# Two more products of a fused attention and tanh-shrink layer computed in two levels, with their factors made on the way

## The chip, the cores and the metric

The kernel runs on one core of one Trainium2 chip. The metric is the device time of one execution in microseconds (us). Three runs of the kernel before took 666.34, 666.99 and 667.07 us; their median, 666.99 us, is the time before. All tensors are 32-bit floats.

## The reference, cut to what matters

```
# linear attention with decay, blocks of 64 along the sequence; B=4, H=8, S=768, D=64
intra = (q_b @ k_b^T * Dmask) @ v_b              # Dmask[i,j] = lam^(i-j) for i >= j
inter = (q_b * lam^(pos+1)) @ kv_state
out_b = intra + inter
kv_state = lam^block * kv_state + (k_b * lam^(block-1-pos))^T @ v_b
# then, on x = the heads side by side, 3072 rows x 512
h = x @ w_in                                     # 512 x 2048
g = h - tanh(h)
result = g @ w_out                               # 2048 x 512
```

The factor that multiplies k before it goes into the state (`lam^(block-1-pos)`) is called k's decay below.

## The kernel before, in words

The sequence is cut into six groups (g = 0 to 5) of 128 positions; with four batches a group has 512 rows, as four chunks b = 0 to 3. The kernel's own attention block is 128 positions.

**Products.** Both matrix products of the layer ("up", x @ w_in, and "down", g @ w_out) are done as seven products of half-size blocks instead of eight, P1 to P7, with sums and differences of blocks made beforehand and combined afterwards (`FACT` names the two operands of each). In `up(g, u, n)` (L449) product n of a quarter u of the hidden columns is four matmuls of 256 columns; the tanh and the subtraction follow in `finish`. `down(g, n)` (L622) is one product of the down projection as one level: 16 matmuls of 256 columns, in four steps u. `down_twice(g, n, zw)` (L675) does the same product in two levels: the block is cut in quarters again, and seven steps x = 1, 2, 6, 5, 7, 3, 4 of four matmuls of 128 columns are run, with three sums (s1, s2 and a21) made by `sums_twice` (L667) on VectorE, a fourth one (a12 -= s2, L691) between steps, a copy by ScalarE after steps 1, 6, 7 and 4 (L689), and two adds at the end (L696, L697). `TWICE` lists the products done in two levels: P3 to P7 of "down" in all groups from 1 on (P3 not in the last). P1 and P2 of "down" are one-level.

**Inner products.** From group 2 on (`GI = 2`), "up" P2 and P4 are done in two levels as well, for all four u at once, by `inner_steps` (L530): "in 2" and "in 4". They run at the end of the group before: "in 2" step by step in turn with the steps of "down" P3, then the stage called the **P4 stage** here: the steps of "in 4" with P1, P6 and P5 of u = 0 of the next group between them.

**Stages of a group from 2 on.** (1) "up" for u = 0 to 3, with the transposes of the next group's chunks 0 and 1 and, after "down" P1, their scores; (2) "down" P1 inside u = 3, then P2; (3) attention output and state of chunks 0 and 1; (4) "down" P4 and P5; (5) scores, P6, output and state of chunks 2 and 3; (6) P7, then P3 with "in 2", then the P4 stage.

**Attention.** `att_transpose` (L323) turns q and k by 32x32 transposes on VectorE (L331, from blocks that SyncE's DMA queue loads in 128-byte pieces, L143) and multiplies q by the powers of lam (L342); `att_scores` makes q k^T on TensorE and masks on VectorE (L356); `att_state` decays k on VectorE (`att_decay`, L361), multiplies by v, and updates the state with two VectorE operations (L379, L380); `att_out` (L384) multiplies state and scores. The PSUM results go to ScalarE (L410).

**Factors of w_out.** Group 0 computes the sums of w_out blocks and stores them to two tensors in memory: `factors` (one level) and `fine` (the second level for the five products of `TWICE`). Later each step loads its 256 KB factor by `piece` (L588), which GpSimd's DMA queue (POOL) issues in a fixed order (`stream`), up to seven (`RING = 7`) ahead; a load waits until the buffer of the seventh piece before it is free.

**Order of work.** A scheduler puts the instructions of each engine in an order; instructions wrapped in `tc.keep_in_program_order` (or `tied(True, ...)`) keep theirs. Each engine runs its queue in order. The banks of PSUM that matter: y banks `ya` and `yb`, `w`, `z`, one buffer each, and four for attention. The pool `sums` has four buffers.

Of the kernel before, what the change touches and what calls it, by code (L numbers as in the profile page):

```python
# [18 lines left out]
BLK = 128  # L19
GB = 2  # L20
# [4 lines left out]
def kernel(  # L25
# [91 lines left out]
    lam_blk = fwd[:, :, BLK - 1:BLK][:, None, :, :].to_broadcast([128, 2, NP, D])  # L117

# [67 lines left out]
    TWICE = (3, 5, 6, 4, 7)  # L186
# [65 lines left out]
    def sums_out(kt):  # L252
# [8 lines left out]
        for n, j in ((1, 0),) if kt % 2 == 0 else ((2, 0), (3, 1)):  # L261
            tied(kt > 1, nc.gpsimd.dma_start(out=fine[:, SUB.index(n), :, kt // 2, :].rearrange("n p c -> p n c"),
                                             in_=y[:, 1:6, ts(j, 128)]))
# [98 lines left out]

    def att_state(g, bs):
# [4 lines left out]
        for n, b in enumerate(bs):  # L368
            kd, vn = raw[g, b]["k"], raw[g, b]["v"]
            if g > 0:  # L370
                att_decay(g, b)
# [6 lines left out]
        if g > 0:  # L378
            nc.vector.tensor_tensor(st, st, lam_blk, op=AL.mult)  # L379
            nc.vector.tensor_tensor(st, st, kv, op=AL.add)  # L380
        else:
            tied(True, nc.scalar.activation(st, kv, AF.Copy))
# [66 lines left out]
    def up(g, u, n):  # L449
# [14 lines left out]
        def finish(c, src):  # L464
            th = work.tile([128, 2, HB], F32, name="th", tag="th")
            nc.scalar.activation(th, src, AF.Tanh)  # L466
# [6 lines left out]
        elif g >= GI and n == 5:  # L473
            nc.scalar.activation(dst(22), z, AF.Copy)
# [10 lines left out]
        elif n == 6:  # L485
            nc.scalar.activation(dst(12), y, AF.Copy)
# [15 lines left out]
    INNER = (2, 4)  # L502
    toks = {}
# [4 lines left out]
    def inner_weights(u):  # L508
        for n in INNER:
            a11, a12, a21, a22 = (a_quarter(n, u, i, k) for i in range(2) for k in range(2))  # L510
            t = late["pool"].tile([128, 4, 128], F32, name="ws2", tag="sums", bufs=4)
# [6 lines left out]
    def inner_tokens(g):  # L518
        for n in INNER:
            x = xt[g][FACT[n][1]]  # L520
            b11, b12, b21, b22 = (x[:, k, ts(j, 128)] for k in range(2) for j in range(2))
            t = late["pool"].tile([128, 4, 128], F32, name="tt2", tag="sums", bufs=4)
# [7 lines left out]
    def inner_steps(g, n, tag):  # L530
# [4 lines left out]
        for x in STEPS:  # L535
# [9 lines left out]
            if x in (1, 4, 6):  # L545
                nc.scalar.activation({1: c11, 4: c21, 6: c12}[x], d, AF.Copy)  # L546
            elif x == 5:
                nc.scalar.activation(r5, dst, AF.Copy)
# [12 lines left out]
    def twice(g, n):  # L561
        return n in TWICE and not (g == NG - 1 and n == 3)

# [7 lines left out]
    def pieces_of(g):  # L571
        if g >= GI:
            yield from ((g, ("in", 4), x) for x in (6, 5, 3))
# [13 lines left out]

    def piece(g, n, x):  # L588

        i = stream.index((g, n, x))  # L590
        while sent["n"] < min(i + RING, len(stream)):
            g_, n_, x_ = stream[sent["n"]]
            t = late["pool"].tile([128, 2, 256], F32, name="wb", tag="wb", bufs=RING)
            if isinstance(n_, tuple):
# [27 lines left out]
    def down(g, n):  # L622
# [16 lines left out]
        if n == 1:  # L639
            res[g, 1] = otile("q1")  # L640
            nc.scalar.activation(res[g, 1], t, AF.Copy)
        elif n == 4:
            res[g, 4] = otile("q4")
            nc.scalar.activation(res[g, 4], t, AF.Copy)
# [22 lines left out]
    def sums_twice(g, n):  # L667
        a11, a12, a21, a22 = quarter(g, n)
        s1, s2 = (late["pool"].tile([128, NU, 128], F32, name=f"s{x}", tag="sums", bufs=4) for x in (1, 2))
        nc.vector.tensor_tensor(s1, a21, a22, op=AL.add)  # L670
        nc.vector.tensor_tensor(s2, s1, a11, op=AL.subtract)
        nc.vector.tensor_tensor(a21, a11, a21, op=AL.subtract)
        low[g, n] = (s1, s2)

    def down_twice(g, n, zw):  # L675
        a11, a12, a21, a22 = quarter(g, n)
        s1, s2 = low.pop((g, n))
        y = bank("y2", "ya" if n in (4, 6, 3) else "yb", 1)[:, 0:128]
        zw = bank("zw", zw, 1)
        o = res[g, n] = otile(f"q{n}")  # L680
        for x, a, dst, keep in ((1, a11, y, o[:, 0:128]), (2, a12, zw[:, 0:128], None), (6, s2, y, o[:, 128:256]),
                                (5, s1, zw[:, 256:384], None), (7, a21, y, o[:, 384:512]), (3, a12, zw[:, 128:256], None),
# [5 lines left out]
            if keep is not None:  # L688
                nc.scalar.activation(keep, dst, AF.Copy)  # L689
            if x == 2:  # L690
                nc.vector.tensor_tensor(a12, a12, s2, op=AL.subtract)  # L691
# [6 lines left out]
        if n == 6:  # L698
# [18 lines left out]
    def down_end(g):  # L717
# [4 lines left out]
        for tag, m, c0, c1 in (("z", 0, 0, 256), ("w", 1, 0, 128), ("ya", 1, 128, 256)):  # L722
# [156 lines left out]
    up(1, 0, 1)  # L879
    for g in range(1, NG):  # L880
        last = g == NG - 1
        p0, p1 = attention(g + 1) if not last else ([], [])
        for u in range(NU):
            for n in (2, 6, 5, 7, 1, 4, 3) if g < GI else (1, 7, 3) if u == 0 else (6, 5, 1, 7, 3) if u + 1 < NU else (
# [5 lines left out]
                else:  # L890
                    every(down(g, 1))
                if g == 1 and u < 2 and n == 5:
                    sums_in(u + 2)
            if g == GI - 1:
                inner_weights(u)
            if not last and u > 1:
                run(p0[u - 2:u - 1])
        if twice(g, 4):
            sums_twice(g, 4)
        every(down(g, 2))  # L900
        run(p0[2:])
        sums_twice(g, 5)
        every(down_twice(g, 4, "z") if twice(g, 4) else down(g, 4))
# [3 lines left out]
        every(down_twice(g, 5, "w"))  # L907
        run(p1[1:2])
        if twice(g, 7):
            sums_twice(g, 7)  # L910
        every(down_twice(g, 6, "z"))
# [3 lines left out]
        every(down_twice(g, 7, "w") if twice(g, 7) else down(g, 7))  # L915
# [47 lines left out]
```

## Time and profile before

The profiled execution took 667.09 us, 0.10 above the median of the runs; its span on the core is 665.3 us, so 1.8 us lie outside the span.

| engine | busy us | share of the span | instructions |
|---|---|---|---|
| TensorE matmul (PE) | 653.6 | 98% | 4992 |
| TensorE weight load (PEld) | 594.6 | 89% | 4992 |
| VectorE (DVE) | 480.0 | 72% | 869 |
| ScalarE (ACT) | 215.0 | 32% | 413 |
| GpSimd (POOL) | 196.0 | 29% | 340 |

DMA moved 121.74 MB. One 32-bit matmul appears as two records in the profile, so the eight records of a step of "down" P3 to P7 are its four matmuls. Ends of matmuls are modelled and overlap the next start, so what a step takes is read from one start to the next, not from its duration. The busy share of an engine is a mean over stages with different limits; the stages around P1 and P2 are the ones to read here.

### The profile page before, as it was taken

What the parts mean: (1) busy time and instruction counts of PE and PEld (TensorE: products, weight loads), DVE (VectorE), ACT (ScalarE), POOL (GpSimd) and SP (SyncE); (2) the same over time, 40 slices, a digit from 0 to 9 for tenths busy, and PEclk for the clock granted to TensorE, in tenths of its full rate; (3) what the DMA queues carried; (4) which work ended last, traced back from release to release, by engine and by line L of the source; (5) the groups of instructions that cost most, each with busy time, mean ns of one, the idle gap of its engine ahead of it and who ended that gap; (6) DMA issues with size and microseconds to landing.
All of it is one profiled execution on the core that took longest, in us unless ns stands there. A gap on an engine that the chain in (4) does not pass through costs nothing.

```text
span 665.3 us, 13244 instructions
## 1 busy us (share of the span) xinstructions
PE 653.6 (98%) x4992; PEld 594.6 (89%) x4992; DVE 480.0 (72%) x869; ACT 215.0 (32%) x413; POOL 196.0 (29%) x340
## 2 busy tenths in 40 slices
PE   7899999999999999999999999999999999999998
PEld 6688888888888899888999988999988899988897
DVE  4467888997787994579895379887368877357753
ACT  4787933423321112341112342112243112233110
POOL 0001425783112445001435101254300245400261
PEclk9999999999999999999999999999999999999999
DMA  9999946997346979435899643698830676610495
GB/s 209 221 209 255 282 159 198 349 332 221 81 87 150 268 214 292 81 71 115 219 265 273 149 76 72 164 297 247 218 68 16 160 237 216 222 38 1 114 303 169
DMA packets 161006, 121.74 MB, mean 183 GB/s; under 512 B 133872, under 2 KB 135024, under 8 KB 160944
## 3 DMA queue, kind: packets, MB, share of 16 engines
q0 software_dynamic: 26400, 86.27, 41.0%
q1 hardware_dynamic: 134400, 34.64, 26.0%
q8 instruction: 39, 0.64, 0.4%
q14 instruction: 23, 0.19, 0.1%
q10 hardware_dynamic: 144, 0.00, 0.0%
HBM read 100.67 MB, written 20.19 MB: 182 GB/s over the span
## 4 chain that ended last, share of the span: by engine, by line
PE 74%; issue 9%; DVE 6%; DMA 4%; POOL 3%; SPq 2%; ACT 2%; POOLq 0%; DVEq 0%; ACTq 0%
PE y L458 13%; PE y L686 12%; PE zw L686 9%; PE z L458 8%; PE h L741 7%; PE y L542 4%; PE w L633 4%; PE y L633 4%; PE sp L352 3%; PE op L406 2%; PE z L542 2%; PE op L400 1%; PE w L542 1%; PE end L725 1%; DMA fine<-wt 1%
## 5 line engine op out<-in xcount | busy, mean ns | idle before, releaser
L598 POOL DMA_DIRECT2D wb<-fine x168 | 90.5, 538 | 137.3 <-PE y L686 60.8
L466 ACT ACTIVATE th<-g 128x512 f32<-128x512 f32 x76 | 47.6, 630 | 99.5 <-DVE g L471 34.2
L689 ACT ACTIVATE q<-y 128x128 f32<-128x128 f32 x96 | 26.6, 278 | 149.3 <-PE y L686 148.5
L458 PE MATMUL y<-xt,w 128*128 128x256 f32 x320 | 73.5, 380 | 0.0
L601 POOL DMA_DIRECT2D wb<-factors x44 | 23.8, 542 | 165.0 <-PE y L633 127.8
L458 PEld LDWEIGHTS y<-xt,w 128*128 128x128 f32 x320 | 59.9, 190 | 8.5 <-ACT g L546 0.9
L467 DVE TENSOR_TENSOR g<-g,th 128x512 f32<-128x512 f32 x76 | 52.1, 689 | 21.1 <-ACT th L466 21.0
L686 PE MATMUL y<-wb,g 128*128 128x128 f32 x456 | 60.6, 278 | 0.0
L741 PE MATMUL h<-xt,w 128*128 128x256 f32 x256 | 58.0, 383 | 2.5 <-DVE w L296 2.5
L741 PEld LDWEIGHTS h<-xt,w 128*128 128x128 f32 x256 | 47.7, 190 | 10.3 <-DVE w L296 2.9
L686 PEld LDWEIGHTS y<-wb,g 128*128 128x128 f32 x456 | 55.1, 192 | 1.3 <-issue 0.3
L686 PE MATMUL zw<-wb,g 128*128 128x128 f32 x304 | 40.3, 275 | 0.1
L458 PE MATMUL z<-tt,ws 128*128 128x256 f32 x160 | 38.1, 381 | 0.0
L458 PE MATMUL y<-tt,ws 128*128 128x256 f32 x160 | 37.8, 379 | 0.0
L458 PE MATMUL z<-xt,ws 128*128 128x256 f32 x160 | 37.8, 379 | 0.0
L686 PEld LDWEIGHTS zw<-wb,g 128*128 128x128 f32 x304 | 37.0, 192 | 0.2 <-DVE g L691 0.2
L633 PE MATMUL w<-wb,g 128*128 128x256 f32 x160 | 35.8, 382 | 0.0
L633 PE MATMUL y<-wb,g 128*128 128x256 f32 x160 | 35.3, 379 | 0.0
L356 DVE TENSOR_TENSOR ss<-sp,mask 128x512 f32<-128x512 f32 x48 | 31.1, 685 | 5.8 <-PE sp L352 5.8
L458 PEld LDWEIGHTS z<-xt,ws 128*128 128x128 f32 x160 | 30.4, 190 | 4.1
L633 PEld LDWEIGHTS y<-wb,g 128*128 128x128 f32 x160 | 30.4, 190 | 4.1
L633 PEld LDWEIGHTS w<-wb,g 128*128 128x128 f32 x160 | 30.1, 190 | 4.4
(178 smaller groups left out, 1292.8 us busy)
## 6 DMA issues: line engine op xcount, KB each, us to landing
wb<-fine POOLq DMA_DIRECT2D x168, 256.0 KB, 4.0
wb<-factors POOLq DMA_DIRECT2D x44, 256.0 KB, 4.3
v_nat<-in_v_dram SPq DMA_DIRECT2D x24, 256.0 KB, 5.2
wb<-fine_in POOLq DMA_DIRECT2D x24, 256.0 KB, 4.2
k_nat<-in_k_dram SPq DMA_DIRECT2D x20, 256.0 KB, 5.0
raw<-in_moe_w_out_dram POOLq DMA_DIRECT2D x10, 512.0 KB, 5.4
raw<-in_moe_w_in_dram SPq DMA_DIRECT2D x8, 512.0 KB, 6.1
raw<-in_moe_w_in_dram SPq DMA_DIRECT2D x16, 256.0 KB, 6.1
```

Of the source, the lines that this page charges most:

```text
L352: tied(g == 0, nc.tensor.matmul(out=sp[j][:, p, :], lhsT=kt[ts(j, 64), p, :], rhs=qt[ts(j, 64), p, :], start=True, stop=True))
L356: tied(g == 0, nc.vector.tensor_tensor(ss[:, j], sp[j], mask[:, j], op=AL.mult))
L458: nc.tensor.matmul(out=t[:, m, :], lhsT=wt[:, kt, ts(m, 128)], rhs=x[:, kt, :], start=first and m == 0 and kt == 0, stop=kt == 1, skip_gro ...
L466: nc.scalar.activation(th, src, AF.Tanh)
L467: nc.vector.tensor_tensor(dst(c), src, th, op=AL.subtract)
L542: nc.tensor.matmul(out=dst[:, ts(u, 128)], lhsT=a, rhs=b, start=x in (1, 2, 5) and u == 0, stop=True, skip_group_check=True)
L598: nc.gpsimd.dma_start(out=t.rearrange("p m c -> p (m c)"), in_=fine[TWICE.index(n_), SUB.index(x_)].rearrange("p u c -> p (u c)"))
L601: nc.gpsimd.dma_start(out=t, in_=factors[XAT[FACT[n_][1]]][:, 2 * x_:2 * x_ + 2, :])
L633: nc.tensor.matmul(out=t[:, m, :], lhsT=a[:, u, kt, ts(m, 128)], rhs=wb[:, kt, :], start=first and u == 0 and m == 0 and kt == 0, stop=u = ...
L686: nc.tensor.matmul(out=dst, lhsT=a[:, u, :], rhs=wb[:, ts(u, 128)], start=x in (1, 2) and u == 0, stop=u == NU - 1, skip_group_check=True)
L689: nc.scalar.activation(keep, dst, AF.Copy)
L741: tied(u == 0, nc.tensor.matmul(out=hm[c][:, m, :], lhsT=w1[u][:, i, a, ts(m, 128)], rhs=xt[0, t][:, i, :], start=m == 0 and i == 0, stop= ...
```

## The change: what it does

- "down" P1 and P2 of groups 2 to 5 go through `down_twice` (in group 1 they stay one-level). Their three sums get tiles of their own in the pool `sums` (`s3`, and `s4` for step 3), since the operands of P1 and P2 are still read elsewhere. P2 ends by adding P1's result and storing; the P4 to P7 banks `w` and `z` swap.
- Their second-level factors do not exist yet, so `factors_twice` makes them once, for group 2: eight quarter loads, eight VectorE subtractions, and fourteen writes to `fine`, all on POOL's DMA queue in the place of the P4 stage of group 1 and of the first steps of group 2. The quarters pass through the ring of `piece`.
- The transposes of chunks 0 and 1 of the group after next move into the P4 stage (two `att_transpose` calls after P1 and P6 of u = 0), and their scores from after P1 to after u = 1.
- k's decay for groups 2 to 4 goes from VectorE (one operation for each chunk) to ScalarE (eight of 128x64 for each chunk, `decay_steps`), two at a time between products.
- The state update becomes four `scalar_tensor_tensor` instead of two operations on the whole tile.
- Many ScalarE operations from group 2 on are tied to program order.

```diff
-    TWICE = (3, 5, 6, 4, 7)
+    TWICE = (3, 5, 6, 4, 7, 1, 2)
...
+    def decay_steps(g, b):
+
+        x = raw[g, b]["k"]
+        for h in range(H):
+            tied(True, nc.scalar.activation(x[:, h, :], x[:, h, :], AF.Copy, scale=mask[:, h % 2, h // 2, BLK - 1:BLK]))
+            yield
...
-            if g > 0:
+            if g == 1:
                 att_decay(g, b)
...
-            nc.vector.tensor_tensor(st, st, lam_blk, op=AL.mult)
-            nc.vector.tensor_tensor(st, st, kv, op=AL.add)
+            for p in range(NP):
+                nc.vector.scalar_tensor_tensor(out=st[:, :, p, :], in0=st[:, :, p, :], scalar=fwd[:, p, BLK - 1:BLK],
+                                               in1=kv[:, :, p, :], op0=AL.mult, op1=AL.add)
...
     def twice(g, n):
-        return n in TWICE and not (g == NG - 1 and n == 3)
+        return g >= GI if n in (1, 2) else g < NG - 1 or n != 3
...
-            yield from ((g, ("in", 4), x) for x in (6, 5, 3))
+            yield from ((g, ("in", 4), x) for x in (6, 5))
+            if g == GI:
+                yield from ((g, ("quarter", 1), x) for x in range(4))
+            yield g, ("in", 4), 3
+            if g == GI:
+                yield from ((g, ("quarter", 2), x) for x in range(4))
...
+    def factors_twice(g, n):
+
+        at, quarters = fine[TWICE.index(n)], []
+        for x, direct in enumerate((1, None, 2, 3)):
+            quarters.append(piece(g, ("quarter", n), x).rearrange("p m (v c) -> p (m v) c", v=2))
+            if direct:
+                nc.gpsimd.dma_start(out=at[SUB.index(direct)], in_=quarters[x])
+        b11, b12, b21, b22 = quarters
+        t1, t2, t4 = (late["pool"].tile([128, NU, 128], F32, name=f"wt{x}", tag="sums", bufs=SUMS) for x in (1, 2, 4))
+        for x, dst, a, b in ((5, t1, b12, b11), (6, t2, b22, t1), (7, b12, b22, b12), (4, t4, b21, t2)):
+            tc.keep_in_program_order(nc.vector.tensor_tensor(dst, a, b, op=AL.subtract))
+            nc.gpsimd.dma_start(out=at[SUB.index(x)], in_=dst)
+            yield
...
     def down_twice(g, n, zw):
         a11, a12, a21, a22 = quarter(g, n)
-        s1, s2 = low.pop((g, n))
-        y = bank("y2", "ya" if n in (4, 6, 3) else "yb", 1)[:, 0:128]
+        s1, s2, s3 = low.pop((g, n))
+        s4 = late["pool"].tile([128, NU, 128], F32, name="s4", tag="sums", bufs=SUMS) if n < 3 else a12
+        y = bank("y2", "ya" if n in (1, 4, 6, 3) else "yb", 1)[:, 0:128]
...
             if keep is not None:
-                nc.scalar.activation(keep, dst, AF.Copy)
+                tied(True, nc.scalar.activation(keep, dst, AF.Copy))
             if x == 2:
-                nc.vector.tensor_tensor(a12, a12, s2, op=AL.subtract)
+                nc.vector.tensor_tensor(s4, a12, s2, op=AL.subtract)
...
                 else:
-                    every(down(g, 1))
+                    every(down_twice(g, 1, "w") if twice(g, 1) else down(g, 1))
...
+                if g == GI and n in (1, 7, 3) and u == 0 or g == GI and n == 6 and u == 1:
+                    next(making)
+                if not last and u > 1:
+                    for _ in range(2):
+                        next(fading, None)
...
-            if not last and u > 1:
+            if not last and g == 1 and u > 1:
                 run(p0[u - 2:u - 1])
+            if not last and g > 1 and u == 1:
+                run(p0[1:2])
+            if g + 2 < NG and u == (1 if g > 1 else 2):
+                fading = (x for b in (0, 1) for x in decay_steps(g + 1, b))
...
-        every(down(g, 2))
+        every(down_twice(g, 2, "z") if twice(g, 2) else down(g, 2))
...
+        x4 = 0
+        making = factors_twice(GI, 1) if g + 1 == GI else iter(())
         for n in (None, None, 1, None, None, 6, None, None, 5, None):
             if n is None:
                 next(p4)
+                x4 += 1
             else:
                 up(g + 1, 0, n)
+                if g + 2 < NG and n in (1, 6):
+                    att_transpose(g + 2, (n // 6,))
+            if n in (6, 5) or n is None and x4 in (4, 5):
+                next(making, None)
         every(p4)
+        if g + 1 == GI:
+            making = factors_twice(GI, 2)
```

## The prediction

> **What bounds the kernel now.** I read the page's busy times first, then busy times by stage for group 3, then TensorE's instructions in order of time around P1 and P2, then VectorE's in the same stretch.
>
> ```profile
> PE 653.6 (98%) x4992; PEld 594.6 (89%) x4992; DVE 480.0 (72%) x869; ACT 215.0 (32%) x413; POOL 196.0 (29%) x340
> ```
> ```profile
> 368.90:396.00 27.10, 27.10 (x147) 24.06 (x146) 15.55 (x24) 10.57 (x18) 1.63 (x3) 1.00 0.52 111
> 396.00:417.00 21.00, 21.00 (x121) 18.29 (x119) 17.52 (x29) 6.65 (x11) 2.15 (x4) 1.00 0.29 67
> 417.00:428.00 11.00, 11.00 (x131) 9.64 (x129) 11.00 (x20) 1.09 (x2) 2.87 (x5) 1.00 0.54 137
> 428.00:441.00 13.00, 13.00 (x116) 12.85 (x116) 11.28 (x20) 2.04 (x8) 7.00 (x13) 1.00 1.07 289
> 460.00:474.00 14.00, 14.00 (x126) 14.00 (x125) 5.58 (x9) 3.50 (x8) 8.04 (x14) 1.00 0.98 293
> ```
> The columns are stretch, length, then busy PE, PEld, DVE, ACT, POOL, granted clock, DMA share, GB/s. TensorE never pauses in group 3, so time is won only by less TensorE work. The reader should also see VectorE: 11.00 of 11.00 us while P2 and the attention output run, 17.52 of 21 us before that, but only 5.58 of 14 us in P3 and the P4 stage.
>
> ```profile
> 406.30 7.07 PE L633 MATMUL y<-wb,g 128*128 128x256 f32 x32
> 413.20 1.89 PE L458 MATMUL z<-xt,ws 128*128 128x256 f32 x8
> 415.02 2.06 PE L352 MATMUL sp<-qt,kt 64*128 64x128 f32 x32
> 417.01 7.17 PE L633 MATMUL w<-wb,g 128*128 128x256 f32 x32
> 424.11 1.10 PE L400 MATMUL op<-qd,state 64*64 64x128 f32 x32
> ...
> 427.98 1.16 PE L686 MATMUL y<-wb,g 128*128 128x128 f32 x8
> 428.97 1.06 PE L686 MATMUL zw<-wb,g 128*128 128x128 f32 x8
> 429.87 1.06 PE L686 MATMUL y<-wb,s 128*128 128x128 f32 x8
> ...
> 434.33 1.06 PE L686 MATMUL y<-wb,gS 128*128 128x128 f32 x8
> ```
> From start to start: P1 takes 6.90 us (406.30 to 413.20); P2, between two blocks of attention, 7.10; a two-level step 0.893, its first after attention 0.99. The step before attention is longer by 0.10 as well (552.29 to 553.28). So one excursion to attention's smaller tiles and back costs 0.20 us, and P2 itself is 6.90.
>
> ```profile
> 375.27 0.69 DVE L550 TENSOR_TENSOR g<-r,y 128x512 f32<-128x512 f32 x1 [2.34 <-PE y L542]
> 381.40 0.69 DVE L471 TENSOR_TENSOR g<-g,y 128x512 f32<-128x512 f32 x1 [4.62 <-PE y L458]
> 428.79 0.69 DVE L380 TENSOR_TENSOR state<-state,kv 128x512 f32<-128x512 f32 x1
> 430.07 0.69 DVE L691 TENSOR_TENSOR g<-g,s 128x512 f32<-128x512 f32 x1 [0.59 <-PE zw L686]
> 430.76 1.06 PE L686 MATMUL zw<-wb,s 128*128 128x128 f32 x8
> ```
> VectorE waits 2.34 and 4.62 us in the P4 stage and just after it, and after the full stretch it waits for TensorE again at 430.07.
>
> **The change, part by part.**
>
> *P1 and P2 in two levels.* Seven steps of 0.893 are 6.25 us against 6.90: 0.65 less for each product. Four groups, two products: 5.2 us less TensorE work. The price is from the same shape on the same tiles, so it is not in doubt. By the Trainium skill ("TensorE: Matmul & The Clock Gate", section on LDWEIGHTS) a weight load of 128 columns takes about 107 ns whatever it is used for; a two-level product has 56 loads, an estimate of 5.97 us if loads alone set its pace, and the sum would be 8 x 0.93 = 7.4. The trace has 0.893 / 8 = 112 ns for a record and PEld at 14.00 of 14.00 in the P4 stage; the row decides.
>
> *Extra excursions.* In the order in which the changed program's instructions stand, P2 of groups 2 to 4 is split: four of the sixteen state products stand after its first step, four after its fifth, the rest at its end. Two more excursions of 0.20 in three groups: +1.2. They fill places where TensorE would wait, so the price may be 0.
>
> *VectorE around P1 and P2.* Added in a group: eight sums of 128x512 at 0.60 from start to start (as the run from 405.46 to 409.04 has six operations in 3.58 us) and four half adds at 0.35 to 0.42: 6.3 us. Taken out of the stretch: the six operations of the transposes, 3.6, two decays, 1.2, and about 0.3 of the state update. Net +1.2 us, where TensorE has 1.3 less. I laid the new order of the three engines along TensorE's starts, from u = 1 of group 3 to P4. TensorE's waits: P7 of u = 3 for ScalarE's copy of P6 (behind two decays), 0.2; the first step into bank z of P2 for the add that empties it (L500 in the new order after three subtractions), 0 to 0.4; P2's step 3 for its sum s4, whose buffer is free only after step 7, 0 to 0.3. I take 0.4 in groups 2 to 4 and 0.5 in group 5, which has no attention products to put in the gap: +1.7. Bounds 0 and 1.2 a group.
>
> *Transposes moved.* Six operations, 3.6 us, into the two VectorE waits above. Behind them in VectorE's queue stands the add of "in 4" step 7 (L550), for which step 4 waits: with them it ends at 377.2, and TensorE gets there at 377.6. Cost 0. SyncE's queue keeps its instructions and their order; the blocks of chunk 1 are issued until 360.9 and land 4 to 5 us later, 9 us before they are needed (6 us in group 2). If they were late, VectorE would stop and TensorE's step 4 with it, one for one. The load of the last k block starts some 30 us earlier, when DMA is at 0.5.
>
> *Decay on ScalarE.* 96 activations of 128x64, not shown in the trace: at most 0.28 (L689, 128x128), at least 0.16 (the smallest VectorE copy, 64x4). Two with one copy make 0.84 at most in the 1.79 us between copies (429.17 to 430.96). Cost 0, hidden by ScalarE's idle time; uncovered, it would be up to 27 us. ScalarE now waits for k's landing in its queue with the copies behind it. For chunk 3 k is issued at 427.6, lands in 3.9 us, and is wanted at about 434.8. VectorE loses twelve decays.
>
> *State update.* Four `scalar_tensor_tensor` of 128 columns: no such row; 0.20 (L525, spacing at 128x128) to 0.49 (L274) each, 0.8 to 2.0 against 1.2 to 1.4 for the two before. I take 1.0, nearest to L525. Nothing on TensorE waits for it for 15 us.
>
> *Loads.* 24 more pieces, 0.54 us of POOL each (13 us of its 469 idle) and 6.3 MB. A piece is issued when the step seven before ends, lands 4.0 to 4.4 us later, and is needed six steps, 5.4 us, after: 1.0 us of cover, as P4 to P7 have now without waiting in groups 2 to 5. If landing took 6.2 us, as in the busiest stretch of group 1 (DMA share 1.13), each wait would be near 0.8.
>
> *Making the factors, once.* POOL's queue: eight quarter loads (0.54 to 0.89 each), fourteen writes at 0.54 to 0.67, among them writes that wait for a quarter to land, with the next loads queued behind. Along the queue: quarters at 257.2, the third piece of "in 4" at 264.2 instead of 257.2, landed by 268.8 and needed at 270.1; the last quarter at 276, landed by 280.4. VectorE's eight subtractions are 4.8 us; with them the add that empties z for P5 of u = 1 ends 0.3 late. +0.3; from 0 to 4 if quarters land in 6.2 us (three landings in a row).
>
> Sum on the profiled execution: 667.09 - 5.2 + 1.2 + 1.7 + 0.3 = 665.1; the median of the runs is 0.1 lower, so 665.0.
>
> **Rivals.** (A) *The full gain*: excursions and waits fall into each other, 666.99 - 5.2 = 661.8. For it: the excursions stand where TensorE would wait. Against it: 0.20 is measured at every excursion. (B) *VectorE becomes the bound* (the other side): where VectorE has no slack from u = 3 to P4, P4 comes when VectorE's added 1.2 us are done, not 1.3 earlier. Three groups at +1.2 and none won in group 5: 670.6. It decides once TensorE's waits around P1 and P2 pass 1.3 us in a group. For it: 11.00 of 11.00. Against it: VectorE had caught up at 430.07. (C) *POOL's in-order queue in group 2*: +3.5 on the forecast, 668.5. (D) *No change*: waits of 0.9 instead of 0.4 a group and excursions at full price, 665.0 + 2 = 667. (E) *No gain from two levels*: excluded by 6.25 against 6.90.
>
> **How the numbers follow.** Forecast (664.0 to 665.6) 0.42, A 0.12, D 0.23, B 0.15, C 0.08. About 0.2%, 1.3 us, is what can be told from no change: faster is below 665.7, slower above 668.3. Faster 0.42 + 0.12 = 0.54; D is the same, 0.24 with the edge of C; slower 0.22. The range runs from A (661.8, cut to 662.2) to half way into B (669.2). The forecast's own range is 664.0 to 665.6.
>
> **What would show it right or wrong.** P1 and P2 as seven steps of 0.89; the matmul's busy time down by about 4 us; two excursions inside P2 with 0.2 around each; VectorE with no idle time of note from u = 3 to P4 and TensorE's waits there named after VectorE's z add (L500) and s4; in the P4 stage no wait named after a transpose or a block load; in group 2 no wait of TensorE on a load. It is wrong if TensorE waits more than 1 us a group around P1 and P2, or on DMA in group 2.

## The result, and the profile after

The changed kernel takes 674.78 us, the median of four runs (671.8 to 678.2); the kernel before, run beside it, 667.03. The ratio is 1.0109, with a 95% interval of 1.0075 to 1.0143: 1.1% slower, where 665.0 had been forecast and 662.2 to 669.2 given as the range. The profiled execution took 676.76 us (span 675.0), so it is one of the slower ones of a kernel whose runs now differ by 1% (before, by 0.4%): it accounts for 9.7 us of span, where the medians differ by 7.8.

The page's first part and its chain of work, after:

```profile
PE 657.1 (97%) x5184; PEld 598.7 (89%) x5184; DVE 500.9 (74%) x929; ACT 242.9 (36%) x537; POOL 222.2 (33%) x386
...
PE 52%; issue 18%; DMA 14%; POOL 6%; SPq 3%; DVE 3%; ACT 3%; POOLq 0%; DVEq 0%; ACTq 0%
```

On the chain that ended last, TensorE had 74% before and DMA 4%. Now DMA has 14% and POOL 6%: loads have come onto the path. (The busy time of PE is no measure of the work: the rows of a slower clock and of broken-up steps count in it.)

The stretches of group 3 that answer to those shown of before, each 5.7 to 6.9 us later; the columns are the same (stretch, length, then busy PE, PEld, DVE, ACT, POOL, granted clock, DMA share, GB/s):

```profile
374.60:401.70 27.10, 27.10 (x169) 23.95 (x168) 19.14 (x31) 10.08 (x17) 1.63 (x3) 1.00 0.54 113
401.70:423.00 21.30, 21.30 (x124) 18.73 (x123) 18.33 (x31) 10.77 (x30) 3.64 (x7) 1.00 0.40 97
423.00:434.00 11.00, 11.00 (x154) 10.00 (x152) 10.63 (x19) 2.71 (x7) 4.33 (x9) 1.00 0.73 213
434.00:447.00 13.00, 12.66 (x112) 12.50 (x111) 11.53 (x23) 5.23 (x21) 6.88 (x14) 1.00 0.92 268
466.90:480.40 13.50, 13.50 (x123) 13.50 (x122) 5.26 (x9) 3.50 (x8) 7.03 (x14) 1.00 0.90 261
```

TensorE seems busy all along, as before, except in P4 and P5 (12.66 of 13.00). P1 and P2 have not become shorter, although they have less to do. Where the 9.7 us of span went is best seen from the starts of the same products in both kernels. Starts are taken from TensorE's instructions in order of time; a group begins with its first up product.

| stretch (us) | before | after |
|---|---|---|
| group 2: start to P4 | 59.10 | 63.14 |
| group 2: P4 to the next group | 45.83 | 47.54 |
| group 3: start to P4 | 59.11 | 59.38 |
| group 3: P4 to the next group | 45.82 | 46.42 |
| group 4: start to P4 | 58.18 | 58.41 |
| group 4: P4 to the next group | 44.94 | 44.94 |
| group 5: start to the last product | 78.01 | 80.75 |

The differences add up to 9.6. Three things stand in the table: P1 and P2 bring nothing (+0.2 to 0.3 from a group's start to P4, where 0.5 less was forecast), group 2 has a stall of 3.8 us of its own (63.14 against group 3's 59.38), and from P4 on groups 2 and 3 are late by 1.7 and 0.6, and group 5 by 2.5 of its 2.7 (27.58 us from P4 to the last product, 25.05 before).

**P1 in group 3.** TensorE and ScalarE in order of time (start, length, engine, line, tiles; in brackets the idle time before and what ended it; of PEld only the rows that waited):

```profile
415.33 1.06 PE L718 MATMUL zw<-wb,g 128*128 128x128 f32 x8
416.10 1.29 ACT L472 ACTIVATE th<-g 128x512 f32<-128x512 f32 x2 [1.45 <-DVE g L482]
...
416.22 1.95 PE L718 MATMUL zw<-wb,s 128*128 128x128 f32 x16
417.29 0.57 ACT L365 ACTIVATE k_nat<-k_nat,mask 128x64 f32<-128x64 f32 x2
417.77 0.26 ACT L721 ACTIVATE q<-y 128x128 f32<-128x128 f32 x1
...
418.08 1.16 PE L718 MATMUL y<-wb,s 128*128 128x128 f32 x8
...
419.07 0.60 PE L464 MATMUL z<-xt,ws 128*128 128x256 f32 x2
419.27 0.28 ACT L721 ACTIVATE q<-y 128x128 f32<-128x128 f32 x1 [1.25 <-PE y L718]
419.60 0.97 PEld L718 LDWEIGHTS y<-wb,s 128*128 128x128 f32 x8 [0.33 <-ACT q L721]
...
421.12 0.97 PEld L718 LDWEIGHTS y<-wb,g 128*128 128x128 f32 x8 [0.33 <-ACT q L721]
```

Step 1 ended at 415.33. Its copy on ScalarE came only at 417.77: ahead of it in ScalarE's queue stood two tanh operations of up product 7, which waited for VectorE until 416.10, and two decays. Step 6 writes the same bank as step 1 and has to wait for that copy. The order in which the scheduler had put TensorE's instructions has steps 2, 5 and 3, all of bank zw, ahead of it (415.33 and 416.22, the latter with both 5 and 3). After them only bank y is left: steps 6, 7 and 4 stand one behind another, each waits for the copy of the one before it, and pieces of up product 3 (two records of eight at a time) are the only filler. From 410.74 to 422.99 P1 and the three up products in it take 12.25 us; less 3 x 1.73 for these, P1 has taken 7.06, where seven steps are 6.25 and one level took 6.90. P2, with attention's products in three pieces, took 8.14 less 1.04 = 7.10, as before to the hundredth.

**The making in group 2.** POOL's, VectorE's and TensorE's rows around the place:

```profile
273.98 0.56 POOL L606 DMA_DIRECT2D fine<-wb  x1 [3.38 <-DMA wb<-factors]
...
275.27 0.56 POOL L611 DMA_DIRECT2D fine<-wt  x1
...
280.65 0.56 POOL L606 DMA_DIRECT2D fine<-wb  x1 [3.53 <-DMA wb<-factors]
281.14 0.69 DVE L610 TENSOR_TENSOR wt<-wb 128x512 f32<-128x512 f32 x1 [1.78 <-DMA fine<-wt]
...
283.56 0.68 DVE L500 TENSOR_TENSOR g<-g,z 128x512 f32<-128x512 f32 x1
...
284.30 2.93 PE L464 MATMUL z<-tt,ws 128*128 128x256 f32 x8 [1.86 <-DVE g L500]
...
287.03 1.48 PE L464 MATMUL y<-xt,w 128*128 128x256 f32 x3
```

POOL's queue waits 3.38 us for a quarter to land, and the write of P1's first sum, made long before, goes out behind it at 275.27. VectorE's first subtraction for P2 (281.14) needs that buffer again and waits for the write; behind it in VectorE's queue stands the add that empties bank z, and TensorE waits 1.86 us for it.

**Late loads.** TensorE's waits for pieces, over the whole run, and POOL's queue at two places:

```profile
PE z L464 <- DVE g L500: 1.9, 1, 1.9
PE end L761 <- DMA wb<-factors: 1.5, 1, 1.5
...
PE y L718 <- DMA wb<-fine: 1.4, 1, 1.4
...
PE zw L718 <- DMA wb<-fine: 0.7, 2, 0.4
```
```profile
323.49 1.59 POOL L628 DMA_DIRECT2D wb<-fine  x3 [2.28 <-PE y L718]
...
660.39 2.12 POOL L631 DMA_DIRECT2D wb<-factors  x4 [2.82 <-PE zw L718]
```

From 426 to 448 a piece took 3.0, 5.1 and 6.0 us to land (least, median, most); 4.5 in the median and 5.5 at most in the same stretch before. Three or four loads that could have gone one at a time went out in a burst, after pauses of 2.3 and 2.8 us. The chain has the second as "657.57 2.80 issue": POOL waited for nothing that the profile shows. The last product's pieces, issued at 660.39, held TensorE up until 664.48. The wait of 1.40 us in P5 of group 2 is not the first pause's: its piece was issued at 328.50, as soon after the step that freed its buffer as others are, and landed 6.4 us later, at 334.91. From 325 to 337 the landings were 3.9, 6.1 and 6.5 us.

### The profile page after: what moved, and what is told of

The parts are those of the page before. It is cut to its first block, busy times and chain, and to the rows that moved or that the text cites. A ratio compares the mean times of both kernels' runs of the same rounds, so it can differ in the third digit from the quotient of the medians.

```text
span 675.0 us, 13953 instructions
## 1 busy us (share of the span) xinstructions
PE 657.1 (97%) x5184; PEld 598.7 (89%) x5184; DVE 500.9 (74%) x929; ACT 242.9 (36%) x537; POOL 222.2 (33%) x386
## 4 chain that ended last, share of the span: by engine, by line
PE 52%; issue 18%; DMA 14%; POOL 6%; SPq 3%; DVE 3%; ACT 3%; POOLq 0%; DVEq 0%; ACTq 0%
PE y L718 13%; PE y L464 11%; PE zw L718 9%; PE z L464 8%; PE y L549 3%; DMA wb<-fine 3%; POOL wb L628 3%; DMA wb<-factors 3%; DMA raw<-in_moe_w_in_dram 3%; PE sp L350 2%; DMA raw<-in_moe_w_out_dram 2%; PE z L549 2%; PE op L412 1%; DMA fine<-f 1%; SPq L141 1%
## 5 line engine op out<-in xcount | busy, mean ns | idle before, releaser
L628 POOL DMA_DIRECT2D wb<-fine x224 | 120.5, 539 | 269.9 <-PE y L718 194.1
L718 PE MATMUL y<-wb,g 128*128 128x128 f32 x584 | 79.1, 278 | 0.1
L718 PEld LDWEIGHTS y<-wb,g 128*128 128x128 f32 x584 | 71.9, 192 | 4.1 <-ACT q L721 1.3
L718 PE MATMUL zw<-wb,g 128*128 128x128 f32 x368 | 49.0, 276 | 0.1
L718 PE MATMUL y<-wb,s 128*128 128x128 f32 x320 | 43.4, 278 | 0.2
L718 PE MATMUL zw<-wb,s 128*128 128x128 f32 x320 | 41.9, 275 | 0.0
L718 PEld LDWEIGHTS y<-wb,s 128*128 128x128 f32 x320 | 38.9, 192 | 1.7 <-ACT q L721 0.7
L718 PEld LDWEIGHTS zw<-wb,s 128*128 128x128 f32 x320 | 38.8, 192 | 0.0
L464 PEld LDWEIGHTS z<-tt,ws 128*128 128x128 f32 x160 | 29.8, 193 | 7.3 <-DVE g L500 3.5
L464 PEld LDWEIGHTS y<-tt,ws 128*128 128x128 f32 x160 | 29.8, 190 | 4.1
```

The costliest lines, as they stand in the source:

```text
L464: nc.tensor.matmul(out=t[:, m, :], lhsT=wt[:, kt, ts(m, 128)], rhs=x[:, kt, :], start=first and m == 0 and kt == 0, stop=kt == 1, skip_gro ...
L628: nc.gpsimd.dma_start(out=t.rearrange("p m c -> p (m c)"), in_=fine[TWICE.index(n_), SUB.index(x_)].rearrange("p u c -> p (u c)"))
L718: nc.tensor.matmul(out=dst, lhsT=a[:, u, :], rhs=wb[:, ts(u, 128)], start=x in (1, 2) and u == 0, stop=u == NU - 1, skip_group_check=True)
```

## The experiments

Ratios are to the kernel before, run on the same chip, with their 95% intervals. "P1 + P2" is taken in group 3 of each profiled execution, from P1's first step to attention's second products, less the three up products (5.19) and attention's first products (1.04); seven plus seven steps would be 12.50. For the kernel before it is P1's 6.90 and P2's 7.10. The two columns after it are the stretches of the table above.

| kernel | ratio | P1 + P2 | group 2 to P4 | group 2 from P4 |
|---|---|---|---|---|
| before | 1 | 14.00 | 59.10 | 45.83 |
| changed | 1.0109 [1.0075, 1.0143] | 14.16 | 63.14 | 47.54 |
| one_level | 1.0016 [0.9994, 1.0038] | one level | 59.11 | 45.87 |
| no_making | 1.0036 [1.0015, 1.0056] | 14.17 | 59.38 | 46.37 |
| no_copies | 1.0047 [1.0028, 1.0066] | 13.66 | 60.48 | 46.86 |
| p1_last | 1.0057 [1.0035, 1.0079] | 14.74 | 61.04 | 45.87 |
| make_later | 1.0096 [1.0058, 1.0134] | 14.17 | 61.65 | 46.72 |
| sums5 | 1.0070 [1.0044, 1.0097] | 14.30 | 61.53 | 46.01 |
| ring8 | 1.0024 [1.0010, 1.0039] | 14.17 | 59.58 | 45.87 |
| c_all | 1.0009 [0.9992, 1.0025] | 14.00 | 59.74 | 45.87 |
| e_x1 | 0.9985 [0.9968, 1.0001] | 13.61 | 60.00 | 45.86 |
| e_best | 0.9956 [0.9930, 0.9982] | 13.06 | 59.48 | 45.86 |
| one_ring8 | 0.9988 [0.9973, 1.0004] | one level | 59.11 | 46.25 |
| order_only | 0.9990 [0.9978, 1.0001] | 13.06 | 60.29 | 47.35 |

### All but P1 and P2 (one_level)

```diff
-        return g >= GI if n in (1, 2) else g < NG - 1 or n != 3
+        return False if n in (1, 2) else g < NG - 1 or n != 3
```
and without the quarters' pieces and the calls of `factors_twice`.

> The changed kernel with P1 and P2 in one level again, as before the change, and without the making of their factors; the moved transposes, k's decay on ScalarE, the fused state update and the tied orders stay. Theory 1 (all of the loss is in the two-level P1 and P2, their factors and their loads): 667 us, within 1 us of the kernel before. Rival (the parts that were moved cost something themselves, for instance copies of ScalarE held up behind decays): 669 us or more, up to the 674.8 of the changed kernel.

Measured: 668.93 against 668.33, 1.0016 [0.9994, 1.0038]. From a group's start to P4 it takes 59.11, 59.10 and 58.18 us in groups 2 to 4, the kernel before to 0.01. Without the making, the moved transposes, the decays on ScalarE and the fused state update cost nothing that shows; the loss is in the two-level P1 and P2 and what they need.

### Without the making (no_making)

```diff
-                if g == GI and n in (1, 7, 3) and u == 0 or g == GI and n == 6 and u == 1:
-                    next(making)
...
-                                    in_=fine[TWICE.index(n_), SUB.index(x_)].rearrange("p u c -> p (u c)"))
+                                    in_=fine[TWICE.index(n_) % 5, SUB.index(x_)].rearrange("p u c -> p (u c)"))
```

> The changed kernel without the making of the factors of P1 and P2 in group 2: both products read the pieces of products 3 and 5 instead, so the output is not the reference's; pieces, steps and loads are as many. In the trace of the changed kernel group 2 takes 4.0 us more than before from its first product to P4, with TensorE waiting 1.86 us for the add that empties bank z, and 1.7 more from P4 to its end. Theory (the making holds VectorE up on a buffer whose write stands in POOL's queue, and TensorE behind it at half clock): 3.8 us less than the changed kernel, 671.0, and up to 5.5 less, 669.3, if the loads that come late in group 2 are due to it as well. Rival (VectorE is late there through the transposes or the loads): 673.5 or more, and the wait at the add stays.

Measured: 670.59, 1.0036 [1.0015, 1.0056], as the theory had it. Group 2 takes 59.38 to P4, as group 3 does (59.37), and the wait for the add to bank z is gone. The stall is the making's, 3.76 us of the profiled execution, and 1.2 of the late loads that follow it in group 2. P1 and P2 stay at 14.17.

### Without the partial copies (no_copies)

```diff
-            if keep is not None:
-                tied(True, nc.scalar.activation(keep, dst, AF.Copy))
+            if keep is not None and (n > 2 or x == STEPS[-1]):
+                tied(True, nc.scalar.activation(keep, dst, AF.Copy) if n > 2 else nc.scalar.activation(
+                    o.rearrange("q (i c) -> q i c", i=4), dst[:, None, :].to_broadcast([128, 4, 128]), AF.Copy))
```

> The changed kernel without ScalarE's three partial copies in P1 and P2: only after the last step is the bank copied, to all four quarters, so the output is not the reference's. In the changed kernel's group 3, P1 takes 7.06 us and P2 7.10 (attention's products taken out) where seven steps are 6.25; steps 6, 7 and 4 of P1 stand one behind another in one bank and each waits 0.33 us for the copy. Theory (these waits for the copies eat the gain): P1 and P2 come to 6.3 to 6.6 us each, 0.5 to 0.8 less for each product, 4 to 6 us less in all: 669 to 671. Rival (VectorE's sums and its add to bank z set the pace): the waits turn into waits for VectorE and the time stays above 673.

Measured: 671.38, 1.0047 [1.0028, 1.0066]. That is 0.4 us above the theory's range as it stands, and inside it, at 670.1, on the scale where the kernel before has 667.0 (beside this run it had 668.33); it is well under the rival's. The theory is half right: P1 fell from 7.06 to 6.48 (408.80 to 420.47, less 5.19), but P2 stayed at 7.18. There a wait for VectorE had taken the copies' place:

```profile
426.07 0.45 PE L406 MATMUL op<-qd,state 64*64 64x128 f32 x8
426.78 1.16 PE L718 MATMUL zw<-wb,s 128*128 128x128 f32 x8 [0.26 <-DVE s L724]
427.87 0.89 PE L406 MATMUL op<-qd,state 64*64 64x128 f32 x24
```

Step 3 of P2 waits for its sum s4, with a piece of attention's products ahead of it and the rest behind. So P1's loss is the copies, P2's is s4. The copies act in two ways that this run does not part: as waits, and through the scheduler, which without them has put the steps of banks y and zw in turn.

### P1 behind the last up product (p1_last)

```diff
-                    6, 5, 7, 1, 3):
+                    6, 5, 7, 1, 3) if not twice(g, 1) else (6, 5, 7, 3, 1):
```

> The changed kernel with P1 written behind the last up product of u = 3 in groups 2 to 5, instead of ahead of it. ScalarE's order is that of the program, so the copy of P1's step 1 no longer stands behind the tanh operations of up product 7 (in group 3 it came 2.4 us after the step's end), and TensorE's order has the steps into bank zw between those into bank y again. Theory (the order of copies sets P1): 0.4 to 0.8 us less in each of four groups, 1.6 to 3.2 in all: 671.6 to 673.2. Rival (VectorE is the bound there): no change, 674 to 675.

Measured: 672.01, 1.0057 [1.0035, 1.0079]: in the expected range as it stands (670.7 on the scale where the kernel before has 667.0), but not for the reason given. P1 and P2 got worse in group 3, 14.74, with a wait of 0.65 us for a piece in P2; the up products no longer stretch P1 while P2's pieces land. In group 4, without such a wait, they take 13.86, 0.26 less than in the changed kernel (14.12). Most of what was won is group 2's stall (61.04) and the loads from P4 on (45.87).

### The making later, a fifth sums buffer, an eighth piece (make_later, sums5, ring8)

```diff
-                if g == GI and n in (1, 7, 3) and u == 0 or g == GI and n == 6 and u == 1:
+                if g == GI and (n in (7, 3) and u == 0 or n in (6, 5) and u == 1):
```

> The changed kernel with the four subtractions that make P2's factors moved one product later in group 2 (behind up products 7 and 3 of u = 0 and 6 and 5 of u = 1), so that in VectorE's queue the first of them, which waits for a buffer whose write to memory was queued on POOL, stands behind the add that empties bank z. Without the making at all, group 2 took 59.4 us to P4 instead of 63.1 and the whole run was 5 us shorter on its scale than the changed kernel. Theory (it is the place of that one waiting subtraction in VectorE's queue): group 2 comes to at most 60.5 us to P4, and the time to 671 to 672.5. Rival (the making's loads, writes and VectorE work are too much for group 2 wherever they stand): group 2 stays above 62 us and the time at 673.5 or more.

Measured: 673.97, 1.0096 [1.0058, 1.0134], not told apart from the changed kernel. In group 2 1.5 us were won to P4 (61.65), not the 2.6 expected: the one wait had become two of 0.9 us, one for ScalarE (L480) and one for VectorE (L500). Both stand behind k's decay, which the change had moved to ScalarE:

```profile
296.38 0.59 ACT L365 ACTIVATE k_nat<-k_nat,mask 128x64 f32<-128x64 f32 x2 [4.36 <-DMA k_nat<-in_k_dram]
...
297.50 1.99 PE L464 MATMUL z<-xt,ws 128*128 128x256 f32 x8 [0.93 <-ACT g L480]
...
302.82 1.99 PE L464 MATMUL z<-tt,ws 128*128 128x256 f32 x8 [0.93 <-DVE g L500]
```

SyncE's queue issues the load of this k tile at 291.78, and it lands at 296.36; without the making it was issued at 285.73 (one_level), and ScalarE did not wait. While ScalarE waits, the copy that empties bank z and a tanh that VectorE needs stand behind the decay. In the changed kernel the same wait is 2.13 us and costs TensorE nothing, since TensorE is late already. No run here puts the decay back on VectorE with the making in place. The profiled execution then lost 4 us in its last product; the last section shows it.

```diff
-    SUMS = 4
+    SUMS = 5
```

> The changed kernel with five buffers instead of four for the sums that P1 to P7 and the making share. Theory: P2's step 3 need not wait for step 7 to free s4's buffer, so P2 falls from 7.1 us to 6.6 to 6.9 in four groups (1 to 2 us in all), and the making's fifth tile no longer waits for a write, so that group 2 loses its 3.8 us: 669 to 671. If only P2 is helped: 673 to 674. Rival (the buffers bind nothing): 674.8, P2 unchanged.

Measured: 672.40, 1.0070 [1.0044, 1.0097]. Group 2 gained 1.6 us, not the 3.8 of the theory, and P2 nothing (7.24 in group 3): the buffer was not what made s4 late.

```diff
-    RING = 7
+    RING = 8
```

> The changed kernel with eight pieces loaded ahead instead of seven: each piece is issued one step, 0.9 us, earlier. Theory (TensorE's waits for pieces of P4, P5 and the last product, some 4 us in the profiled run, come from issues that a landing of 5 to 6 us or a pause of 2 to 3 us in POOL's queue makes late): the waits of 0.3 us go, those of 1.4 and 1.5 fall to 0.5, 2 to 4 us less in all: 671 to 673. Rival (the DMA engines are full there, and an earlier issue only waits longer): 674 or more.

Measured: 669.85, 1.0024 [1.0010, 1.0039], more than the theory had asked. TensorE's waits in the whole run:

```profile
PE h L777 <- DVE w L294: 3.0, 3, 1.6
PE sp L350 <- ACT kt L336: 2.6, 3, 1.2
PE idle L313 <- POOL ident masks.py:199: 1.4, 1, 1.4
PE tp L334 <- DMA k_nat<-in_k_dram: 1.1, 2, 0.6
PE end L761 <- DMA wb<-factors: 0.7, 1, 0.7
PE acc L807 <- DVE s L816: 0.6, 1, 0.6
PE kv L379 <- DMA v_nat<-in_v_dram: 0.4, 1, 0.4
```

No wait for a piece of P4 or P5 is left, and the one for bank z in group 2 is gone too: with one buffer more in the ring, POOL's queue writes P1's first sum at 273.45 instead of 275.27, and VectorE finds its buffer free. Groups 2 and 3 take 45.87 us each from P4, within 0.05 of before the change. That P1 and P2 bring nothing is untouched (14.17).

### All of these together (c_all)

P1 last, the making later, and:

```diff
-    SUMS = 4
+    SUMS = 5
...
-    RING = 7
+    RING = 8
...
-    late["blk"] = ctx.enter_context(tc.tile_pool(name="blk", bufs=2 * B - 1))
+    late["blk"] = ctx.enter_context(tc.tile_pool(name="blk", bufs=2 * B - 2))
```

The last line makes the room for the two buffers.

> P1 behind the last up product, the making of P2's factors one product later, five buffers for sums, eight pieces ahead, and six instead of seven buffers for attention's blocks, which makes the room. If the three causes (ScalarE's copies, the making, late loads) are the whole loss and add up, 674.8 less 2.4, 3.5, 1 and 2: about 666, level with the kernel before or 1 us ahead. Rival (VectorE, with over 18 of 20 us busy from u = 3 to P4, becomes the bound as soon as the others go): 668 to 669, with TensorE's waits from u = 3 to P4 named after VectorE.

Measured: 668.58, 1.0009 [0.9992, 1.0025], the kernel before again and no more. The 668.58 is the rival's number only as it stands: on the scale of the expectation, where the kernel before has 667.0 (beside this run it had 668.18), it is 667.4, between the theory's 666 and the rival's 668, so the time does not decide. P1 and P2 are at 14.00. But the copy of P1's step 1 stood behind a tanh of up product 3 on ScalarE (copy at 411.51, the step had ended by 409.9), and P2's s4, ready to be made when its product began, came at 419.64, behind three operations of line L650 in VectorE's queue. Both are matters of order, not of VectorE's time, and the next two kernels mend them.

### The order of the copies, and of s4 (e_best, e_x1)

```diff
@@ the order at u = 3, down_twice for n = 1 in two parts
-                    6, 5, 7, 1, 3) if not twice(g, 1) else (6, 5, 7, 3, 1):
-                if n != 1:
+                    6, 5, 7, 1, 3) if not twice(g, 1) else (6, 5, 7, 0, 3, 1):
+                if n == 0:
+                    down1 = down_twice(g, 1, "w")
+                    next(down1)
+                elif n != 1:
@@ sums_twice (e_best alone)
+        s4 = a12
+        if n < 3:
+            s4 = late["pool"].tile([128, NU, 128], F32, name="s4", tag="sums", bufs=SUMS)
+            nc.vector.tensor_tensor(s4, a12, s2, op=AL.subtract)
```

> The last combination (P1 behind the last up product, making later, five sums buffers, eight pieces ahead, six block buffers), and two orders mended: P1's step 1 and its copy stand ahead of up product 3, so that the copy is not behind the tanh of that product on ScalarE, and the sum s4 of P1 and P2 is made with the other sums, not after step 2. TensorE's order of instructions is then step for step the alternation of banks y and zw in both products, with attention's products in one piece behind P2. Theory (the gain of 0.65 us a product is there and is lost to the order of the copies and of s4): from u = 3 to P4 another 1.0 to 1.4 us less in each of four groups than in the last combination, which was 0.1% above the kernel before: 662.5 to 664.5 on the scale where that kernel has 668.2, 0.5 to 0.8% below it. Rival (VectorE is the bound): less than 0.4 us a group, waits named after VectorE in their place, and the time within 0.2% of the kernel before.

> The last combination with the first of the two orders alone: P1's step 1 and its copy ahead of up product 3; s4 stays where it was. Theory: P1 falls to 6.3 to 6.5 us, P2 stays at 6.9 to 7.1; 0.5 to 0.7 us less in each of four groups, 665.5 to 666.5. Rival (VectorE is the bound): no change, 668 to 669.

Measured: e_best 664.55 against 667.85, 0.9956 [0.9930, 0.9982], faster than both kernels, by 0.4% than the one before; e_x1 667.25, 0.9985 [0.9968, 1.0001]. Both gained somewhat less than the theory had asked. TensorE and ScalarE in e_best, group 3:

```profile
411.37 1.05 PE L721 MATMUL zw<-wb,g 128*128 128x128 f32 x8
...
412.08 0.25 ACT L724 ACTIVATE q<-y 128x128 f32<-128x128 f32 x1
412.39 1.16 PE L721 MATMUL y<-wb,s 128*128 128x128 f32 x8
...
413.38 1.06 PE L721 MATMUL zw<-wb,s 128*128 128x128 f32 x8
413.58 0.28 ACT L724 ACTIVATE q<-y 128x128 f32<-128x128 f32 x1 [0.49 <-PE y L721]
414.28 1.06 PE L721 MATMUL y<-wb,s 128*128 128x128 f32 x8
415.17 1.06 PE L721 MATMUL zw<-wb,s 128*128 128x128 f32 x8
```

Each copy now runs beside a step of the other bank. Step 6 (412.39) still comes 0.13 us late, after the first copy, which stands behind two tanh operations as before; from 413.38 on the steps follow one another in 0.89 us. With e_x1, P1 is 6.71 and P2 6.90; with s4 made early as well P2 falls to 6.35 (416.95 to 424.34, less 1.04). From the start to P4, group 3 takes 58.28 us and group 4 57.11, where before they took 59.11 and 58.18: the gain of the two levels is 0.8 to 1.1 us a group. VectorE is busy 41.24 of 44.00 us in group 3 (396 to 440) and does not stop it. Group 2 gains nothing: P1 and P2 take 14.01 there, with a wait of 0.93 us for VectorE's add L500, and ScalarE has waited 3.29 us for k ahead of it, as in make_later.

### The two levels on and off with loads in time, and the order alone (one_ring8, order_only)

one_level with the ring of ring8, and the changed kernel with the two orders of e_best:

```diff
@@ one_ring8, on one_level
-    RING = 7
+    RING = 8
@@ order_only, on the changed kernel
+        s4 = a12
+        if n < 3:
...
-                    6, 5, 7, 1, 3):
+                    6, 5, 7, 1, 3) if not twice(g, 1) else (6, 5, 7, 0, 3, 1):
```

> P1 and P2 in one level, no making, and eight pieces loaded ahead. It is the partner of the run with eight pieces ahead and two levels (0.24% above the kernel before). Theory (two levels in the order of the changed kernel are worth nothing even where the loads are in time): level with the kernel before, within 0.15%, so faster than its two-level partner by 0.1 to 0.3%. Rival (two levels do bring their gain and the loads alone hide it): slower than the partner.

Measured: 666.82, 0.9988 [0.9973, 1.0004]. One level with eight pieces ahead is level with the kernel before and 0.36% ahead of ring8, its two-level partner: in the order of the changed kernel two levels are worth less than one, whatever the loads do. With e_best's order, loads and buffers they are ahead of it by 0.3% (the two intervals just overlap).

> The changed kernel with the two mended orders alone (P1's step 1 and its copy ahead of up product 3, the rest of P1 behind it; s4 made with the other sums), with seven pieces ahead, four sums buffers and the making where the change put it. TensorE's order from P1 to attention's products is the one of the best combination. Theory (two losses that do not replace each other: the order of copies and sums takes the gain of P1 and P2, and seven pieces ahead are too few for group 2's making and for the loads of P2, P4, P5 and the last product): P1 and P2 gain about 1 us a group over the changed kernel where no piece is late, and the waits for pieces and the stall in group 2 stay: 0.2 to 0.6% above the kernel before, where the changed kernel is 1.1% above. Rival (the order is the whole loss): level with the best combination, 0.3% or more below the kernel before.

Measured: 667.20, 0.9990 [0.9978, 1.0001], between the two expectations: the order alone takes back the whole loss of 1.1%, though stalls in group 2 (60.29 and 47.35) are still seen in its profiled execution, which took 671.23 us. The stall to P4 is no longer the one of the changed kernel: TensorE's 1.86 us at bank z are not there, and its waits of 0.59 and 0.94 us stand behind ScalarE's wait of 4.02 us for k. The causes do not add: with the order mended, what seven pieces ahead, four sums buffers and the making's place still cost is about the 0.3% to e_best, whose interval just overlaps.

## Why the prediction was wrong, step by step

- *P1 and P2 in two levels, 5.2 us less*: the price of a step was right. In e_best the steps follow in 0.893, and P1 and P2 take 13.06 in group 3 and 12.83 in group 4 instead of 14.00, where 12.50 had been counted; in group 2 they take 14.01. In the changed kernel nothing of it arrived, which is rival E, excluded by the price of a step: the price holds for a step, not for the order in which steps stand.
- *VectorE around P1 and P2, +1.7* and *extra excursions, +1.2*: the steps that failed. Together they left 0.65 x 2 - 0.4 - 0.4, some 0.5 us a group; P1 + P2 came out 0.16 longer. The waits were looked for on VectorE (the add L500, s4), and of ScalarE's copies only that of up product 6 was named, 0.2. The prediction reads the changed program's order for P2 (where the attention products stand); the same order has steps 5 and 3 of P1 ahead of 6, which means that 6, 7 and 4 stand alone in one bank and each waits for a copy. This was not worked out. It cost 0.58 us a group in P1 by no_copies. The wait for s4 in P2 was named rightly, but "its buffer is free only after step 7" was not its reason: a fifth buffer did nothing, an earlier place in the program ended it.
- *Loads, 0*: failed. The 1.0 us of cover rested on landings of 4.0 to 4.4 us; around P4 the median was 5.1 and the most 6.0 in group 3, 6.1 and 6.5 in group 2, and POOL paused for 2.3 and 2.8 us. The bound that was worked out for 6.2 us, waits near 0.8, was the nearer end. From P4 on the profiled execution lost 1.7 us in group 2, 0.6 in group 3 and 2.5 in group 5; with an eighth piece ahead 1.7, 0.6 and 1.5 of these are gone.
- *Making the factors, +0.3 (0 to 4)*: mis-sized at the far end, 3.76. The mechanism is rival C's (3.5): POOL's queue, in order, behind landings. What the working left out is where it comes to bear, a subtraction in VectorE's queue that waits for a buffer whose write is late. Once that wait is out of the way, a second one shows, ScalarE's for a k tile whose load is issued later (make_later, e_best, order_only).
- *Transposes, decay and state update, 0*: right by one_level, that is, without the making. With it, the wait that the prediction named for k's decay, "with the copies behind it", does come in group 2: 2.1 us of ScalarE's time in the changed kernel, hidden there, and up to 4.4 in the later ones, where TensorE loses 0.4 (c_all) to 1.9 us (make_later) behind it. The rest came out as counted: four operations of the state update took 1.12 us (1.0 forecast), and two decays 0.57 on ScalarE, 0.28 each, the upper end. (The 0.49 taken as the upper bound for a state operation, L274, is a mean over two shapes: its 128x128 operations take 0.28, its 128x512 ones 0.69.)
- *Rival B, VectorE becomes the bound*: not so. Its 670.6 was nearest in size, but e_best wins about 1 us in groups 3 and 4 each, with VectorE at 41.24 of 44.00 in group 3.
- Of the signs that were to show it wrong, both came: over 1 us a group of loss around P1 and P2 (14.16 against 12.50), and a wait on DMA in group 2 (1.40). The longest waits in P1 are named after ScalarE's copies (0.33 each), not after VectorE as had been expected.

## What to carry to other kernels

A faster sequence of steps that share one accumulator and copy it out between them runs only as fast as the copies come back, so look at the queue of the engine that copies, and at whether another bank's step stands between any two: if the order uses that filler up early, the gain is gone. Halving the length of steps doubles the rate at which pieces are asked for; a ring that covered landings with 1 us to spare should get its extra buffer in the same change. And a one-time preparation that shares queues and buffers with the main loop is priced by the first instruction that waits for a buffer or a load, and by what is queued behind that.

## What had not been expected of the hardware

A wait of under 2 us brought TensorE to half its clock. Granted clock is the third column from the end, for the stretch after the 1.86 us wait in group 2 of the changed kernel, and, below, for the last product of make_later, which began with waits of 1.66 and 0.87 us for pieces:

```profile
286.00:288.00 2.00, 2.00 (x6) 1.53 (x6) 1.97 (x4) 0.73 (x2) 0.94 (x2) 0.50 1.03 332
```
```profile
664.00:666.00 2.00, 2.00 (x6) 1.56 (x6) 0.00 (x0) 0.00 (x0) 0.00 (x0) 0.50 0.05 16
666.00:668.00 2.00, 2.00 (x6) 1.60 (x5) 0.00 (x0) 0.00 (x0) 0.00 (x0) 0.50 0.00 0
668.00:670.00 2.00, 2.00 (x13) 1.86 (x12) 0.42 (x1) 0.00 (x0) 0.00 (x0) 0.68 0.00 0
```

In group 2 the next two up products, 1.73 us each elsewhere, were 2.73 and 2.51 from start to start, so that a wait of 1.86 cost 3.6. In make_later the last product took 11.4 us from its first record, with the second wait in it, instead of 7.3. Waits of 1.40 (group 2, P5) and 1.49 us (the last product of the changed kernel) left the clock at 1.00. The Trainium skill ("TensorE: Matmul & The Clock Gate", Part 1) has the half clock after an idle window of about 3.4 us; here 1.86 us were enough once, and the trace decides.

POOL's pauses of 2.3 and 2.8 us stand at fixed places of its own queue. In all ten kernels here with 386 operations on POOL, one of 2.28 us stands before the 182nd, one of 2.8 or 3.69 before the 282nd and one of 2.8 before the 382nd or 383rd, about 100 operations apart; the first begins anywhere from 314 to 321 us. That speaks for POOL's own queue and against the load of memory at that moment. What POOL does in them stays open: no run took them away by themselves, an eighth piece only covered them.
